# One output tile split into three single-bank tiles, block maxima split in two, and a new written-out order of the work

## The chip, the cores and the metric

The kernel runs on one core of a Trainium2 chip. The metric is the device time in microseconds (us) of one execution. The core has five engines that run side by side, each strictly in its own order: TensorE (PE, matrix products, with its weight loads shown as PEld), VectorE (DVE), ScalarE (ACT), GpSimd (POOL), and SyncE (SP), which here issues all DMAs. TensorE writes its results to PSUM, of which the kernel takes eight banks of 512 fp32 columns on 128 partitions.

## The reference

```python
# attention: q, k, v of (4 batches, 8 heads, 768 positions, 64)
scores = 1/sqrt(64) * q @ k.transpose
mask   = |block_i - block_j| <= 1, or first/last block on either side,
         or the block is one of 3 sampled blocks of its row   # blocks of 32
scores = where(mask, scores, -1e9) - rowmax
attn   = exp(scores) / (sum(exp(scores)) + 1e-9)
x      = (attn @ v) as (3072 tokens, 512)
# feed-forward: w_in (512, 2048), w_out (2048, 512)
h   = x @ w_in
out = (h * clip(h + 3, 0, 6) / 6) @ w_out
```

All arrays are fp32. The kernel keeps fp32 accuracy by splitting operands into a high part of type fp32r and a low part.

## The kernel before, in words

The work is cut into 64 *units*, 64 *steps* and 32 *weights*. They are Python objects whose methods each issue a few instructions, and the names of the methods are used below.

A **unit** `u0` to `u63` is one head of one batch and one half of its 384 query rows. On TensorE it has `m_0 m_1 m_2`, each two 128x384 score products for 128 query rows (384 keys each), from which DVE takes block maxima (`r_0 r_1 r_2`, one reduction over 768 columns each, 24 blocks of 32); `fin_0` adds the mask to the block maxima and `fin_1` reduces them to one negated row maximum. `mt` transposes that maximum with three small matmuls and `qm` (ACT) copies it into a row of the operand `qb`, so that the score products `s_0 s_1 s_2` (four matmuls each, of `KA,QA` and of `kb,qb`) come out already masked and shifted. From unit 10 on a DMA takes the place of `mt` and `qm`. `e_0 e_1 e_2` are the exponentials (ACT) and `av` the product with the values: in units 0 to 11 it also yields the row sums (12 matmul passes of 128 columns, `av_0 av_1 av_2`), later it runs in half the array. `qh kh qb` (ACT), `ql` (DVE) and `kl` (POOL, 1.8 us) make the high and low parts of the operands; `uc dw uu tt` and `ux` finish the unit's output.

A **weight** `w0` to `w31` is one 128-row chunk of `w_in` or `w_out`: a DMA load, `size` (ACT), `bits_0 bits_1 bits_2` (DVE), `high` (ACT), `low` (DVE), and a DMA that saves the low part to DRAM, from where the steps load it again.

A **step** `m0` to `m63` takes two of the 16 chunks of the feed-forward for one block of 384 tokens; eight steps make a block, and a block of tokens needs eight units. `h_00` to `h_11` are 24 matmuls, `ga gb gh gl` (ACT, DVE, ACT, POOL) the activation and its split, and `o_tj` 18 matmuls that accumulate into three output banks, one for each `t`, over all eight steps. After the last step of a block, `oc_t` (DVE, from bank `t`) and `od_t` (DMA) carry the block out.

**PSUM.** `big` is a pool of two tiles of two banks for `m`, `s`, `h` and a few others; `av` has one bank. The last three banks are one tile, `OUT` (line 370), of 128 x 3 x 512. Bank `t` of it is what `o_tj` accumulates into (line 850). Before the first step needs them, the same banks serve other purposes: `mq` (line 474) uses bank 2, and the `m` of units 1 to 8 (the `early` units, line 630) use banks 0 and 1 in place of a `big` tile, each `m_t` over both of them, so that `m_1` comes after `r_0` has read them and `m_2` after `r_1`.

**What sets the order.** No planner runs in the kernel. The string `SCORE` (line 41) lists all 3537 methods in one written-out order, `play` (line 886) calls them in that order, and every instruction is kept in program order on its engine (line 357, which is why the profile gives L357 for nearly all of them). So one phrase of `SCORE` places work on several engines' queues at once. The framework adds semaphore waits where an instruction touches a tile that another engine still uses.

Of the kernel before, what the change touches and what calls it, by code (L numbers as in the profile page):

```python
# [13 lines left out]
F32 = mybir.dt.float32  # L14
# [27 lines left out]
    u0 loadq loadk; k0 samp table ind ident; u0 loadv; w0 load; w2 load; u1 loadv; u0 qh qb ql kh; k0 index; u1 loadq;  # L42
    k0 allow_0 allow_1; u0 m_0; k0 allow_2; u0 m_1; k0 allow_3 indc; u0 r_0; k0 mq kb_0; w0 size; u0 r_1; k0 rows; w2
    size; k0 identc mqc; u0 kl m_2; k0 qb_00; u0 r_2; k0 qb_11; u1 qh qb; w0 bits_0; u1 loadk; k0 qb_01; w0 bits_1; k0
    qb_10; w0 bits_2; u0 fin_0; w0 high; w1 load; k0 kb_1; u0 fin_1 mt qm; w0 low; u0 s_0; u1 ql; w0 save; u0 s_1; w2
    bits_0; u2 loadq; u0 e_0; w2 bits_1; u1 kh; u0 av_0; w2 bits_2; u0 e_1; u1 kl; w3 load; u1 m_0; w2 high; u0 s_2;
    u1 r_0; w1 size; u0 av_1; w2 low; u2 loadk; u0 e_2; w1 bits_0; w2 save; u2 qh; u1 m_1; w1 bits_1; u0 av_2; u2 qb;
    w1 bits_2; u1 r_1; w1 high; w5 load; u2 loadv; w3 size; w1 low; u1 m_2; u0 dw; u2 ql; w1 save; u0 uc; u1 r_2; u3
    loadq; u2 kh; u1 fin_0; u2 m_0; u1 fin_1; u2 kl; u1 mt; u2 r_0; u1 qm s_0; w5 size; u2 m_1; w3 bits_0; u3 loadk;
    u1 e_0 s_1; w5 bits_0 bits_1; u1 s_2 e_1; w5 bits_2; u1 av_0 e_2; u2 r_1; w4 load; w5 high; w3 bits_1; u2 m_2; u3  # L50
    qh; u1 av_1; w5 low; u3 qb; u2 r_2; w5 save; u3 kh; u1 av_2; u3 ql; u2 fin_0; u4 loadq; u3 m_0; u2 fin_1; u3 kl;
    u1 dw; u3 loadv; u2 mt; u3 r_0; u2 qm; w4 size; u2 s_0; u1 uc; w4 bits_0; u3 m_1; u4 loadk; u2 s_1 e_0; u1 rg; w3
    bits_2; u3 r_1; w6 load; w3 high; u2 s_2; m1 loadout_0; u2 e_1 av_0; w4 bits_1; u2 e_2; w3 low; u3 m_2; w4 bits_2;
    u4 qh; w3 save; u2 av_1; u4 qb; u3 r_2; w7 load; w4 high; u2 av_2; u3 fin_0; u4 kh ql; u1 rc; u5 loadq; u4 kl; u3
    fin_1; w6 size; u1 rs; u3 mt; u4 m_0 loadv; u3 qm; u4 r_0; u2 uc; u3 s_0; u2 dw; u5 loadk; u3 s_1; w6 bits_0; u3
    e_0; w6 bits_1; u4 m_1; u3 e_1 s_2; w6 bits_2; u3 av_0; u4 r_1; w8 load; w6 high; u3 e_2; w6 low; u1 rb; u4 m_2;
    u5 qh; w4 low; u3 av_1; w6 save; u5 qb; u4 r_2; w4 save; w7 size; u3 av_2; u5 kh; u4 fin_0; u5 ql; u4 fin_1; u5
    kl; u6 loadq; u5 m_0; u3 uc; u5 loadv; u4 mt; u5 r_0; u3 dw; u4 qm; u3 rg; u5 m_1; w7 bits_0; w8 size; u4 s_0; u6
    loadk; w7 bits_1; m1 loadin_1; u4 s_1; m1 loadin_0; w8 bits_0; u4 e_0; w8 bits_1; u4 e_1 s_2; w8 bits_2; u4 av_0;
    u5 r_1; u4 e_2; w10 load; u6 qh; u1 ux_0; u5 m_2; u6 qb; u4 av_1; u6 ql; u1 ux_1; u5 r_2; u7 loadq; u6 kh; u4  # L60
    av_2; u5 fin_0; w8 high; u1 ux_2; u5 fin_1; u6 kl; u3 rc; u5 mt; u3 rs; u6 m_0; u4 uc; u6 loadv; u5 qm; u6 r_0;
    w10 size; u5 s_0; u7 loadk; w7 bits_2; u4 dw; u5 s_1 e_0; w10 bits_0; w9 load; u6 m_1; w10 bits_1; u5 e_1 s_2; u6
    r_1; u5 av_0; w7 high; w10 bits_2; u5 e_2; u3 rb; w8 low; u6 m_2; u7 qh; u5 av_1; u6 r_2; w8 save; u7 qb; w11
    load; u7 kh; u6 fin_0; u5 av_2; u7 ql; w10 high; u6 fin_1; u7 kl; u8 loadq; w9 size; u7 m_0 loadv; u5 uc; u6 mt;
    u7 r_0; u6 qm; u5 dw; u8 loadk; u6 s_0; w9 bits_0; u5 rg; w7 low; u6 s_1 e_0; u3 ux_0; w7 save; u7 m_1; u6 e_1
    s_2; w10 low; u6 av_0; u3 ux_1; w9 bits_1; w10 save; u6 e_2; w9 bits_2; u6 av_1; u8 qh; u7 r_1; w12 load; u8 qb
    kh; u3 ux_2; u6 av_2; u8 ql; w9 high; m1 loadout_1; u5 rc; u8 kl; u5 rs; w11 size; u7 m_2; u9 loadq; u8 loadv; u6
    uc; u7 r_2; u6 dw; u9 loadk; u7 fin_0; u8 m_0; u7 fin_1; w11 bits_0; u7 mt qm; u8 r_0; w12 size; u7 s_0; w9 low;
    u8 m_1; u7 e_0 s_1; w11 bits_1; w9 save; u5 rb; u7 s_2; u8 r_1; u7 e_1 av_0; w11 bits_2; u7 e_2; w12 bits_0; w14
    load; u9 kh; u8 m_2; w12 bits_1; u7 av_1; u9 qh; u8 r_2; u9 kl qb; w11 high; u7 av_2; u8 fin_0; u10 loadk; u8  # L70
    fin_1; u9 ql; u8 mt; u7 uc; u9 loadv; w11 low; u8 qm; u9 m_0; u10 loadq; u7 dw; u9 m_1 r_0; w11 save; w14 size; u7
    rg; u9 r_1; u8 s_0; u5 ux_0; u8 e_0 s_1; w12 bits_2; u5 ux_1; u8 s_2; w14 bits_0; w16 load; u8 e_1 av_0; u5 ux_2;
    u10 kh; w14 bits_1; u9 m_2; w14 bits_2; u8 e_2 av_1; u9 r_2; u10 kl; w18 load; u10 qh qb; u7 rc; u8 av_2; u7 rs;
    w12 high; w14 high; u9 fin_0; u11 loadk; u9 fin_1; u10 ql; u9 mt; u8 uc; u10 loadv; w12 low; u10 m_0; u11 loadq;
    u9 qm; u8 dw; u9 s_0; u10 r_0; w12 save; w16 size; w14 low; u9 s_1 e_0; w16 bits_0; w14 save; u9 e_1 s_2; w16
    bits_1; u7 rb; u9 av_0; w18 size; w16 bits_2; u9 e_2; w18 bits_0; w13 load; w18 bits_1; u10 m_1; u11 kh; u10 m_2;
    w18 bits_2; u9 av_1; u11 qh; u10 r_1; u11 kl; w15 load; w18 high; u9 av_2; u11 qb; u10 r_2; w16 high; w18 low; u12
    loadk; u9 uc; u11 loadv; u7 ux_0; w18 save; u9 dw; u10 fin_0; u7 ux_1; u9 rg; w16 low; w13 size; u7 ux_2; w16
    save; w13 bits_0; m0 h_00; w15 size; w13 bits_1; m0 h_10; w13 bits_2; w15 bits_0; w13 high; w17 load; m0 h_01; u10
    fin_1; w13 low; u10 mt; u11 ql; w13 save; m0 h_11; w15 bits_1; u12 loadq; m2 loadin_0; m1 h_00; u9 rc; m0 ga; w15  # L80
    bits_2; u9 rs; w19 load; m1 h_01; w15 high; m0 gb; m2 loadin_1; w15 low; m0 gh; m1 h_10; m3 loadin_0; w15 save;
    w17 size; m0 gl; m1 h_11; u10 s_0; m3 loadin_1; w17 bits_0; m1 ga; u9 rb; m0 o_00; w17 bits_1; m0 o_01; u10 e_0;
    m1 gb; m0 o_10; w19 size; w17 bits_2; u10 s_1; m1 gh; w19 bits_0; w20 load; u10 s_2; w19 bits_1; u10 e_1; m0 o_11;
    w19 bits_2; u12 kh; u11 m_0; m1 gl; w22 load; m0 o_20; w19 high; u11 r_0; w17 high; m0 o_21; m2 loadout_0; u10
    e_2; u11 m_1; w19 low; m2 loadout_1; u10 av_0; u12 qh; u9 ux_0; w19 save; u12 qb; u11 r_1; u12 kl; u11 m_2; u9
    ux_1; u10 av_1; w20 size; u11 r_2; w20 bits_0; u13 loadk; m2 h_00; w20 bits_1; w17 low; m2 h_01; w20 bits_2; w17
    save; w22 size; m2 h_10; u11 fin_0; w24 load; w20 high; w22 bits_0; m4 loadin_0; w22 bits_1; m2 h_11; u11 fin_1;
    w22 bits_2; u11 mt; m1 o_00; m2 ga; w20 low; w21 load; m1 o_01; m4 loadin_1; u12 ql; w20 save; w22 high; m1 o_10;
    m2 gb; u13 loadq; u12 m_0; m1 o_20; w22 low; m2 gh; u12 m_1 r_0; w22 save; w24 size; m2 gl; m1 o_11; m3 loadout_0;
    u12 r_1 m_2; m1 o_21; u12 r_2; u11 s_0; w21 size; m3 loadout_1; w24 bits_0; u11 s_1 e_0; u9 ux_2; u10 av_2; w21  # L90
    bits_0; u11 e_1; w21 bits_1; u11 s_2; w21 bits_2; u10 dw; u12 loadv; m2 o_00; u12 fin_0; w26 load; w21 high; u12
    fin_1; w24 bits_1; u12 mt; u10 uc; m2 o_01; u14 loadv; u13 kh; w24 bits_2; u11 av_0; w21 low; w23 load; u11 e_2;
    u13 kl; w21 save; u11 av_1; w24 high; u13 qh qb; u11 av_2; u13 ql; u14 loadk; w26 size; w24 low; u14 loadq; u12
    s_0; u11 uc; w26 bits_0; w24 save; u15 loadv; u11 dw; u13 m_0; w26 bits_1; m2 o_10; u12 e_0; u11 rg; w26 bits_2;
    m2 o_20; w23 size; u13 r_0; w25 load; m2 o_11; m4 loadout_0; w26 high; w23 bits_0; u13 loadv m_1; w23 bits_1; u12
    s_1; u13 r_1; m2 o_21; u12 e_1; w23 bits_2; u13 m_2; m4 loadout_1; u12 s_2; u13 r_2; w23 high; w28 load; u14 qh;
# [231 lines left out]
def fused_kernel(ctx: ExitStack, tc, qT, kT, vP, sampled, w_in, w_out, krows, table, ident_d, out):  # L328
# [81 lines left out]
    class Masks(Work):  # L410
# [11 lines left out]
        def heat(self):  # L422

            self.hot = sb.tile([P, 2, HALF], F32R, name="ghi")
            nc.gpsimd.memset(self.hot.bitcast(F32), 1.0)

        def warm(self, *number):
            for _ in range(number[-1]):
                pe.matmul(OUT[:, 2, :HALF], lhsT=self.hot[:, 0, :P], rhs=self.hot[:, 1], start=True, stop=True)

# [505 lines left out]
```

## Time and profile before

| | |
|---|---|
| time of 3 runs | 995.15 us median (993.82 to 997.5) |
| the profiled execution's own time | 994.87 us |
| its span, first to last instruction | 993.1 us |
| PE busy | 950.6 us, 96% of the span, 4756 matmuls |
| DVE busy | 642.3 us, 65%, 900 instructions |
| ACT busy | 471.1 us, 47% |
| POOL busy | 249.9 us, 25% |
| mean share of the DMA engines | about 0.75 in the first 160 us, 0.4 to 0.5 after it |

The profiled execution is the one that all rows below come from. Its own time is 1.8 us longer than its span (start and end of the program), and 0.3 us under the median. Busy time of PE overstates its work, since a record lasts until the modelled end of a matmul while the next one has begun. What a matmul costs in a dense row is read from the distance between starts.

### The profile page before, as it was taken

How to read it: one execution, taken by the hardware profiler on the slowest of the kernel's cores; microseconds unless marked ns; L12 is line 12 of the kernel's file. 1: busy time of each engine (PE TensorE's matmuls, PEld its weight loads, DVE VectorE, ACT ScalarE, POOL GpSimd, SP SyncE). 2: the span in 40 equal slices, each digit the busy share in tenths (PEclk: the TensorE clock that was granted, in tenths of full speed). 3: DMA queues.
4: the chain of work that ended last, by engine and by line, in shares of the span. 5: the costliest groups of instructions: out<-in, count | busy, mean ns of one | idle time of the engine just before them, and what ended most of it. 6: DMA issues, size and time to landing. Idle time of an engine off the chain costs nothing.

```text
span 993.1 us, 13262 instructions
## 1 busy us (share of the span) xinstructions
PE 950.6 (96%) x4756; PEld 767.9 (77%) x4756; DVE 642.3 (65%) x900; ACT 471.1 (47%) x712; POOL 249.9 (25%) x148
## 2 busy tenths in 40 slices
...
GB/s 199 193 244 210 273 267 236 202 220 147 144 139 139 123 165 132 155 111 165 142 153 132 131 152 163 124 154 134 170 147 108 149 131 138 145 48 146 142 118 72
DMA packets 103701, 155.48 MB, mean 157 GB/s; under 512 B 32819, under 2 KB 51891, under 8 KB 103636
## 3 DMA queue, kind: packets, MB, share of 16 engines
...
q14 instruction: 28, 0.23, 0.1%
...
## 4 chain that ended last, share of the span: by engine, by line
PE 80%; DVE 12%; ACT 3%; issue 3%; DMA 1%; POOL 0%; DVEq 0%; ACTq 0%
PE big L357 44%; PE out L357 25%; PE av L357 12%; DVE xhl L357 3%; DVE bm L357 3%; DVE acc L357 2%; DVE QA L357 2%; ACT pr L357 1%; ACT xhl L357 1%; DMA win_lo<-xhl 1%; DMA wout_lo<-xhl 1%; DVE wraw L357 0%; ACT qb L357 0%; DVE uu L357 0%; DMA qraw<-qT 0%
## 5 line engine op out<-in xcount | busy, mean ns | idle before, releaser
L357 PE MATMUL big<-xhl,win_hi 128*128 128x384 f32 x1024 | 265.0, 340 | 0.6 <-DVE bm L357 0.6
L357 POOL TENSOR_TENSOR glo<-g,ghi 128x768 fp32r<-128x768 f32 x64 | 120.2, 1878 | 430.3 <-ACT ghi L357 425.1
L357 ACT ACTIVATE pr<-big 128x768 f32<-128x768 f32 x192 | 153.0, 809 | 102.9 <-PE big L357 102.1
L357 POOL TENSOR_TENSOR kb<-kraw,KA 64x768 fp32r<-64x768 f32 x64 | 124.4, 1943 | 298.8 <-ACT KA L357 252.8
L357 PEld LDWEIGHTS big<-xhl,win_hi 128*128 128x128 f32 x1024 | 184.5, 188 | 14.3 <-issue 7.3
L357 DVE TENSOR_REDUCE bm<-big 128x24 f32<-128x768 f32 x168 | 158.0, 953 | 54.8 <-PE big L357 53.0
L357 PE MATMUL big<-xhl,wlo_in 128*128 128x384 f32 x512 | 172.3, 337 | 0.0
L357 PE MATMUL av<-pr,vo 128*64 128x384 f32 (+1 forms) x768 | 163.6, 494 | 0.1
L357 PE MATMUL out<-wout_hi,ghi 128*128 128x512 f32 x384 | 152.7, 398 | 5.8 <-DVE wraw L357 5.8
L357 PE MATMUL out<-wout_hi,glo 128*128 128x512 f32 x384 | 151.2, 394 | 0.6 <-POOL glo L357 0.6
L357 PE MATMUL out<-wlo_out,ghi 128*128 128x512 f32 x384 | 150.8, 393 | 0.0
L357 PE MATMUL big<-QA,KA 128*128 128x384 f32 x384 | 138.5, 361 | 3.1 <-ACT pr L357 1.3
L357 PE MATMUL big<-qb,kb 97*128 97x384 f32 x384 | 132.7, 345 | 3.9 <-ACT qb L357 3.2
L357 DVE SCALAR_TENSOR_TENSOR g<-g,big 128x768 f32<-128x768 f32 x64 | 60.8, 950 | 109.7 <-ACT g L357 109.3
L357 ACT ACTIVATE g<-big,half_b 128x768 f32<-128x768 f32 x64 | 57.7, 902 | 142.5 <-PE big L357 126.9
L357 PEld LDWEIGHTS av<-pr,vo 128*64 128x64 f32 (+1 forms) x768 | 67.6, 147 | 65.6 <-issue 50.5
L357 PE MATMUL big<-KA,QA 128*128 128x384 f32 x336 | 92.7, 367 | 13.9 <-ACT KA L357 5.1
L357 PEld LDWEIGHTS big<-KA,QA 128*128 128x128 f32 x336 | 74.8, 255 | 35.9 <-issue 8.8
L357 DVE TENSOR_TENSOR acc<-pr 128x768 f32<-128x768 f32 x52 | 54.3, 1045 | 68.1 <-ACT pr L357 67.8
L357 PEld LDWEIGHTS big<-xhl,wlo_in 128*128 128x128 f32 x512 | 96.2, 188 | 0.0
L357 PEld LDWEIGHTS big<-QA,KA 128*128 128x128 f32 x384 | 73.9, 192 | 23.8 <-ACT pr L357 7.7
L357 ACT CAST ghi<-g 128x768 fp32r<-128x768 f32 x64 | 53.3, 833 | 73.7 <-DVE g L357 48.5
...
## 6 DMA issues: line engine op xcount, KB each, us to landing
...
```

Of the source, the lines that this page charges most:

```text
L357: return lambda *a, **k: tc.keep_in_program_order(op(*a, **k))
```

## The change

Three things are changed. The tile `OUT` becomes three tiles of one bank each, `out0`, `out1` and `out2`, taken from the pool anew by each use. The `m` of an early unit takes two of these tiles, one for each of its two matmuls, and the pair of banks turns with the unit: units 1 and 2 have banks 1 and 2, units 3 and 4 banks 2 and 0, units 5 and 6 banks 0 and 1, units 7 and 8 banks 1 and 2. Each early `r` becomes two reductions over 384 columns, one a bank. And `SCORE` is another order of the same 3537 methods. Two methods that no `SCORE` calls (`heat` and `warm`) go.

```diff
-    OUT = outp.tile([P, NT, DM], F32, name="out")
...
         def mq(self):
-            self.mqp = OUT[:, 2]
+            self.mqp = outp.tile([P, DM], F32, name="out0")
...
         def m(self, t):
             if self.early:
-                ps = OUT[:, 0:2]
+                bank = (self.n - 1) // 2
+                ps = [outp.tile([P, DM], F32, name=f"out{(bank + 1 + j) % NT}")[:, :HALF] for j in range(2)]
             else:
                 ps = big_tile()
-            self.mps = [*(self.mps if t else []), ps[:, :, :HALF]]
+            self.mps = [*(self.mps if t else []), ps if self.early else ps[:, :, :HALF]]
             for j in range(2):
-                pe.matmul(ps[:, j, :HALF], lhsT=self.QA[:, t:HALF:NT], rhs=self.KA[:, j * HALF:(j + 1) * HALF], start=True, stop=True)
+                out_j = ps[j] if self.early else ps[:, j, :HALF]
+                pe.matmul(out_j, lhsT=self.QA[:, t:HALF:NT], rhs=self.KA[:, j * HALF:(j + 1) * HALF], start=True, stop=True)
 
         def r(self, t):
             if t == 0:
                 self.bm = sb.tile([P, NT, NB], F32, name="bm")
             bm = self.bm[:, t].rearrange("p (j n) -> p j n", j=2)
-            dve.tensor_reduce(out=bm, in_=self.mps[t].rearrange("p j (n e) -> p j n e", e=BLK), axis=AX.X, op=ALU.max)
+            if self.early:
+                for j in range(2):
+                    dve.tensor_reduce(out=bm[:, j], in_=self.mps[t][j].rearrange("p (n e) -> p n e", e=BLK), axis=AX.X, op=ALU.max)
+            else:
+                dve.tensor_reduce(out=bm, in_=self.mps[t].rearrange("p j (n e) -> p j n e", e=BLK), axis=AX.X, op=ALU.max)
...
-                moe_out[self.b, self.hf] = [OUT[:, t_] for t_ in range(NT)]
+                moe_out[self.b, self.hf] = [outp.tile([P, DM], F32, name=f"out{t_}") for t_ in range(NT)]
```

Of the two orders, this is what the engines' queues hold around unit 4 and 5, read from the strings (the diff of the strings themselves is some 570 lines):

```
before  PE   u4.s_0 u4.s_1 u4.s_2 u4.av_0 u5.m_2 u4.av_1 u4.av_2 u5.mt u6.m_0 u5.s_0 u5.s_1 u6.m_1
after   PE   u4.mt u5.m_0 u5.m_1 u4.s_0 u5.m_2 u4.s_1 u4.s_2 u4.av_0 u4.av_1 u4.av_2 u5.mt u6.m_0 u6.m_1 u5.s_0
before  DVE  u5.r_0 w7.bits_0 w7.bits_1 w8.bits_0 w8.bits_1 w8.bits_2 u5.r_1 u1.ux_0 u6.ql u5.r_2 u5.fin_0 u1.ux_2 u5.fin_1 u3.rc u6.r_0
after   DVE  w7.low w8.bits_2 u5.r_0 u5.r_1 u1.ux_0 u5.r_2 u5.fin_0 u1.ux_2 u5.fin_1 w8.low u6.ql w10.bits_0 w10.bits_1 u3.rc w10.bits_2 u6.r_0
after   ACT  u3.uc u4.qm u3.dw w8.high u4.e_0 u4.e_1 u1.ux_1 u4.e_2 u6.qh u6.qb w10.size w9.size u6.kh u4.uc u5.qm
```

The pattern of the new order, `mt` of a unit, then `m_0 m_1` of the next, then `s_0` of the first, with `r_0 r_1` side by side, is the same from unit 1 to unit 8. Up to `u9 s_0` TensorE's queue holds the same 97 methods in both orders, and DVE's holds eight more in the new one (`w14 low`, the four DVE methods of `w16`, `w18 bits_0 bits_1`, `u10 r_0`). Up to `u1 s_0` it holds three more (`w3 bits_0 bits_1 bits_2`). Up to `m7 o_21` TensorE's and ACT's queues hold the same methods in both. The last 17 methods of `SCORE` are the same, in the same order:

```
m62 o_21; m63 o_00 o_01 o_10 oc_0 o_11 od_0 o_20 oc_1 o_21 od_1 oc_2 od_2
```

## Rows read from the trace of the kernel before

**Rows 1.** Busy time by stretch: length, then engine busy (instructions), clock, DMA share, GB/s.

```profile
0.00:29.41 29.41, 17.65 (x59) 12.85 (x59) 18.12 (x35) 16.55 (x27) 10.28 (x23) 0.97 0.66 204
29.41:103.89 74.48, 65.85 (x266) 47.46 (x265) 62.23 (x102) 58.81 (x97) 16.33 (x9) 0.97 0.70 215
103.89:230.25 126.36, 120.07 (x584) 96.74 (x584) 110.21 (x164) 74.70 (x118) 32.08 (x16) 1.00 0.74 238
230.25:993.10 762.85, 747.05 (x3852) 610.84 (x3850) 451.79 (x602) 321.07 (x471) 191.21 (x101) 1.00 0.45 136
```

**Rows 2.** Timeline: first matmul of `u1 s_0`, `u9 s_0` and `m7 o_21`.

```profile
29.41 0.63 PE L357 MATMUL big<-QA,KA 128*128 128x384 f32 x1
...
103.89 0.44 PE L357 MATMUL big<-QA,KA 128*128 128x384 f32 x1 [0.59 <-ACT qb L357]
...
230.25 0.39 PE L357 MATMUL out<-wout_hi,ghi 128*128 128x512 f32 x1
```

**Rows 3.** Chain of waits, pieces without a wait: start, length, what, matmuls.

```profile
79.62 3.87 PE av L357 x12
...
889.72 11.93 PE big L357 x66
...
974.95 10.31 PE out L357 x45
```

**Rows 4.** Who waited for whom, 29.41 to 103.89: total, times, longest.

```profile
PE big L357 <- ACT qb L357: 3.0, 6, 0.6
PE out L357 <- DVE bm L357: 2.0, 2, 1.1
...
DVE bm L357 <- PE out L357: 7.3, 9, 1.4
```

**Rows 5.** Chain of waits around `u4 m_0`, `r_0`, `m_1`.

```profile
56.89 0.36 PE out L357 x2
...
57.28 0.97 DVE bm L357
...
58.29 0.68 PE out L357 x2
```

**Rows 6.** The tile bm: count, shortest, median, longest in ns, first and last start.

```profile
L357 DVE TENSOR_REDUCE mneg<-bm x64: 185/228/230, 14.8 to 874.7; 128x3 fp32r<-128x72 f32 x64
L357 DVE TENSOR_REDUCE bm<-out x24: 948/956/961, 21.7 to 91.0; 128x24 f32<-128x768 f32 x24
```

**Rows 7.** DVE timeline: `bits_0`, two `bits`, and `low` of weights.

```profile
59.43 0.43 DVE L357 TENSOR_SCALAR xhl<-xhl 128x512 int32<-128x512 int32 x1
59.89 1.42 DVE L357 SCALAR_TENSOR_TENSOR xhl<-wraw,xhl 128x512 int32<-128x512 int32 x2
...
70.48 0.69 DVE L357 TENSOR_TENSOR xhl<-xhl,win_hi 128x512 f32<-128x512 f32 x1
```

**Rows 8.** The tile QA on DVE, and the timeline around two `kl` on POOL.

```profile
L357 DVE SCALAR_TENSOR_TENSOR QA<-qraw,QA x64: 555/556/3877, 3.8 to 866.2; 64x384 fp32r<-64x384 f32 x64
...
72.94 1.81 POOL L357 TENSOR_TENSOR kb<-kraw,KA 64x768 fp32r<-64x768 f32 x1 [6.12 <-ACT KA L357]
73.09 2.07 DVE L357 SCALAR_TENSOR_TENSOR QA<-qraw,QA 64x384 fp32r<-64x384 f32 x1
...
56.01 1.82 POOL L357 TENSOR_TENSOR kb<-kraw,KA 64x768 fp32r<-64x768 f32 x1 [6.24 <-ACT KA L357]
```

**Rows 9.** Who waited for whom on PE, 230.25 to the end.

```profile
PE out L357 <- DVE wraw L357: 5.8, 6, 1.7
PE big L357 <- DVE QA L357: 3.6, 3, 1.6
PE big L357 <- DVE bm L357: 1.7, 2, 1.6
```

**Rows 10.** Timeline of the last block's `o_10`, `oc_0`, `o_11`.

```profile
984.86 0.39 PE L357 MATMUL out<-wout_hi,glo 128*128 128x512 f32 x1
...
985.28 0.69 DVE L357 COPY wraw<-out 128x512 f32<-128x512 f32 x1 [7.82 <-PE out L357]
...
986.03 0.50 PE L357 MATMUL out<-wout_hi,ghi 128*128 128x512 f32 x1 [0.78 <-DVE wraw L357]
```

More of the change, by code (lines that the diff above doesn't have):

```diff
@@ L41 @@
 SCORE = """
[L42 to L96, printed above, removed]
@@ L102 @@
-    m4 h_01; u15 kh; u13 sumb; w30 load; w25 high; u15 m_0; m6 loadin_0; u13 av sumc; u15 kl r_0; u14 s_0; u13 tt; u11
-    ux_0; u16 loadk; u17 loadv; m4 h_10; w25 low; u14 e_0; u13 uu; w25 save; u15 m_1; w28 bits_2; m4 h_11; u15 r_1;
-    w27 load; w28 high; m3 o_10; m4 ga; w28 low; u14 s_1; w28 save; m4 gb; m3 o_20; u14 e_1; w26 low; u14 s_2; m5
-    loadout_0; m4 gh; u14 suma; w26 save; u15 m_2; m3 o_11; w30 size; u15 r_2; m4 gl; u16 kh; m3 o_21; m5 h_00; u16
-    qh; m5 loadout_1; u16 qb; w30 bits_0; m5 h_01; u11 ux_1; u15 fin_0 fin_1; u16 kl; u14 e_2; u15 mt; m4 o_00; w27
@@ L107 @@
-    size; m6 loadin_1; m7 loadin_0; u14 av sumb; u17 loadk; u14 sumc; u11 ux_2; m5 h_10; u14 tt; u18 loadv; u16 ql;
-    u14 uu; u17 loadq; m5 h_11; w27 bits_0 bits_1; u16 m_0; m5 ga; m4 o_01; w30 bits_1; m4 o_10; m5 gb; m4 o_20; u16
-    r_0; m5 gh; u16 m_1; m6 loadout_0; m4 o_11; m5 gl; u16 r_1 m_2; m4 o_21; u16 r_2; u15 s_0; w30 bits_2; u15 s_1
-    e_0; u16 fin_0; w29 load; w27 bits_2; m5 o_00; w30 high; u16 fin_1; w31 load; u15 s_2; w27 high; w30 low; u16 mt;
-    m5 o_01; u15 e_1; w27 low; w30 save; m5 o_10; u17 kh; w27 save; u15 suma; m6 h_00; u17 qh kl qb; m6 h_10; u15 e_2;
@@ L222 @@
-    loadk qb; u45 loadv; m31 o_01; u41 sumc tt uu; u43 m_2; m32 h_00; u44 ql; u43 r_2; u45 loadq; m32 h_10; u43 fin_0
-    fin_1; m31 oc_0; u43 mt; m32 h_01; u44 kh; m31 od_0; m32 h_11; m34 loadin_0; u44 kl; m31 o_10; m32 ga; m34
-    loadin_1; m31 o_11; m32 gb; u45 loadk; m31 o_20 oc_1; u44 m_0; m32 gh; m33 loadout_0; u43 s_0; u44 r_0; m31 od_1;
-    m32 gl; m31 o_21; u43 e_0; u44 m_1; m31 oc_2; m33 loadout_1; u43 s_1; u44 r_1; m31 od_2; m32 o_00; u43 e_1; m32
-    o_10; u43 suma s_2; m33 h_00; u43 e_2; u45 kh; u43 sumb; m33 h_01; u45 qh; u43 sumc; m32 o_01; m35 loadin_0; u45
@@ new lines @@
+    size; k0 rows; w2 size; k0 mqc; u0 kl m_2; k0 qb_01; u0 r_2; k0 qb_11 qb_10; w2 bits_0; u1 loadk qh; w2 bits_1; u1
+    qb; k0 qb_00; w2 bits_2; w0 bits_0; w1 load; w2 high; u1 ql; u0 fin_0; u2 loadq; w0 bits_1 bits_2; k0 kb_1; u0
+    fin_1; w0 high; w3 load; u0 mt; u1 kh; w0 low; u0 qm; w2 low; u1 m_0; w0 save; u1 m_1 kl r_0; w2 save; u0 s_0; w1
+    size; u0 s_1 e_0; u1 r_1 m_2; u0 e_1 s_2; u2 loadk; w1 bits_0; u1 r_2; u0 av_0; u2 qh qb ql; u0 e_2 av_1; w1
+    bits_1; u3 loadq; w3 size; w1 bits_2; u0 av_2; u1 fin_0; w1 high; w5 load; u1 fin_1; w3 bits_0; w1 low; u1 mt; u0
@@ new lines @@
+    bits_1; u7 qh; u3 rb; u5 av_1; u7 qb ql; w11 size; w9 bits_2; u8 loadq; u5 av_2; w11 bits_0; w9 high; w12 load;
+    w11 bits_1; u7 kh; w11 bits_2; u6 mt; u7 loadv; u5 uc; u7 m_0; w10 low; w14 load; u7 m_1; u6 qm; u7 kl r_0; w10
+    save; u5 dw; u6 s_0; w11 high; u5 rg; u6 s_1; u7 r_1; u6 e_0; u7 m_2; u8 loadk; u3 ux_0; u6 e_1 s_2; u7 r_2; u6
+    av_0; u3 ux_1; u8 qh; u3 ux_2; u8 qb; u7 fin_0; u6 av_1; u7 fin_1; u6 e_2; w11 low; u8 ql; w12 size; w11 save; u6
+    av_2; w9 low; u9 loadq; w14 size; u5 rc; w9 save; w14 bits_0; u7 mt; u5 rs; u8 kh; w12 bits_0; u8 loadv; w12
@@ new lines @@
+    bits_1; u6 uc; u8 m_0 m_1; u7 qm; u8 kl r_0; u6 dw; u7 s_0; u8 r_1; u7 s_1 e_0; u8 m_2; u9 loadk; w12 bits_2; u7
+    e_1 s_2; u8 r_2; w16 load; w12 high; u7 av_0; u5 rb; u9 qh; u8 fin_0 fin_1; u9 qb ql; u7 av_1 e_2; w14 bits_1; u10
+    loadq; w14 bits_2; u7 av_2; w12 low; w14 high; w18 load; w14 low; w12 save; u9 kh; u8 mt; u9 loadv; w14 save; u7
+    uc; u9 m_0 kl; u8 qm; u9 r_0; u7 dw; u9 m_1; w16 size; u9 r_1; u7 rg; u8 s_0; u10 loadk; u5 ux_0; u8 e_0 s_1; w16
+    bits_0; u5 ux_1; u8 s_2; w16 bits_1; u8 e_1 av_0; w16 bits_2; u10 qh; u5 ux_2; w13 load; w16 high; u10 ql; u9 m_2;
```

488 lines of the change are left out of this document (267 added, 221 removed).

## The prediction, on record before the changed kernel ran

> **What bounds the kernel now.** I first cut the windows view at three places that the two orders share [rows 1], found as instructions in the timeline [rows 2]: `u1 s_0` (29.41 us), `u9 s_0` (103.89) and `m7 o_21` (230.25). The reader is to see that PE is nearly full after 230 us (747.05 of 762.85) and has gaps before. In the second stretch DVE is busy 62.23 of 74.48 us, PE 65.85 by records that overstate it, ACT 58.81: three engines that wait for each other.
>
> PE's own work comes from the dense pieces of the chain of waits [rows 3]: 0.18 us a 384-column matmul (11.93 / 66), 0.23 us a 512-column one (10.31 / 45), 3.87 us for the twelve `av` matmuls of an early unit. An early unit has 12 `s` and 6 `m` matmuls, so 18 x 0.18 + 3.87 = 7.1 us, its three small transposes left out. The second stretch holds eight units: 74.48 / 8 = 9.3 us a unit, of which PE stands 2.2. Then I read who waited there [rows 4]. PE waits for the `qb` copy behind `mt` (3.0 us in 6 waits) and for the maxima (2.0 in 2). DVE waits at `r` for PE's `m` (7.3 in 9).
>
> Last I read PE's waits after 230 us [rows 9]. The largest is for `wraw`, which is `oc`: 5.8 us in 6. The timeline shows what kind of wait it is [rows 10]. The last matmul of `o_10` starts at 984.86, so `o_11` was due at 985.09. It starts at 986.03, as `oc_0` ends. But `o_11` writes bank 1 and `oc_0` reads bank 0. They share only the tile `OUT`, and the wait belongs to the tile. `oc_0` in turn starts only after `o_10`, which it doesn't read.
>
> **The change, part by part.**
>
> *Three tiles for one.* A write to one bank no longer waits for a read of another. At the end both orders hold the same methods, so nothing there but the tiles can take the wait away. Four of the six waits are of this kind in the last two blocks, where PE has no attention work left to put between: 986.03 - 985.09 = 0.94 us each, 3.8 us. What is late next there is `o_21`, then `oc_2` and its DMA, as now. The other two lie inside attention work (the longest 1.7 us [rows 9], so 5.8 - 4 x 0.78 = 2.7 together) and I take half, 1.3. Sum -5.1, between -6.9 and 0 if the wait stays.
>
> *One maximum a bank.* It adds 24 DVE instructions. No row shows a 384-column reduction. From the 72-column one (228 ns) and the 768-column one (956) [rows 6] the slope is 728 / 696 = 1.05 ns a column, so 228 + 312 x 1.05 = 0.55 us each, 1.11 for 0.96. From below it is half of 956, nothing added. I take 0.15 us a pair as the dearer end, 21 pairs in the second stretch: 3.2 us of DVE. In return `m_1` starts sooner. Before, `m_0` to the next pair is 58.29 - 56.89 = 1.40 us, with the maximum of 0.97 between [rows 5]. After, the first half starts 0.18 us sooner, at 57.28 - 56.89 - 0.18 = 0.21, ends at 0.76, and `m_1` may start at 0.80. The second half ends at 1.32, so `m_1` is through at 1.54. PE's own work in that is 4 x 0.18 = 0.72, so the turn costs PE 0.8 us a unit.
>
> The Trainium skill has a rule that weighs here (Perfetto Trace Analysis, Optimizing Scalar/DVE Operations). A DVE instruction has a fixed access cost, about 125 ns on PSUM, so larger operations pay where the engine is saturated. Where it isn't but holds others up, smaller pieces can end the work sooner. By the first half the 21 pairs cost 2.6 us and return nothing, which is the first rival below; by the second the turn counts.
>
> *The new order, first stretch.* DVE now does `w2`, parts of `w0` and `u1 ql` ahead of `u0 fin_1`, some 2.4 us more by the durations of [rows 7]. But `u1 m_0 m_1` stand ahead of `u0 s_0` on PE, and three more `bits` are done by `u1 s_0`. I take 0, from -1 to +2.4.
>
> *Second stretch.* In the new order `m_0 m_1` of the next unit stand between `mt` and `s_0`, so the turn of 0.8 us covers the `qb` copy, which cost up to 0.6 each time. `r_0 r_1` are side by side, so DVE doesn't stop between them, and 5.3 us of PE work (`s`, `m_2`, `av`) lie between `m_2` and `mt`. That gives 7.1 + 0.8 = 7.9 us a unit. I add 0.2 for the small transposes, 0.2 for `m_0` waiting on `kh`, which is late in ACT's queue behind two `size`, and 0.4 for DVE held by POOL. The price of that is in [rows 8]: a `ql` that starts 0.15 us into `kl` takes 2.07 us and not 0.56, 1.5 us more, and I count one in four. 8.7 x 8 = 69.6 us. DVE is the check. By `u9 s_0` it has eight more methods behind it: 0.69 (`w14 low`), 0.43 + 1.42 + 0.69 (`w16`), 0.43 + 0.71 (`w18`), 0.96 (`r_0`), 5.3 us [rows 6, 7]. Three `bits` (1.85) went ahead of the stretch. 62.23 + 5.3 - 1.85 + 3.2 = 68.9. An engine that stood 12.2 us before won't be without a gap, so I take 72: -2.5, between -8.5 (66, halves at half the price) and +6 (every unit held 1.5 us).
>
> *Third stretch.* PE and ACT have the same left, DVE 5.3 us less. DVE is busy 110.21 of 126.36 here and the chain of waits runs mostly over weights. I take 3 of the 5.3. Bounds -5.3 and +2, the latter if the DMA engines, at 0.74, hold the weights instead.
>
> *Fourth stretch.* PE is full, and the other waits on DVE are 3.6 + 1.7 us [rows 9]. An order drawn anew can meet as many others. I take nothing for it, between -3 and +4.
>
> SP's queue is reordered too. No `load` becomes a new wait by name, and the DMA shares of [rows 1] leave room, so I cost it at nothing. If that is wrong it shows as PE waiting for `KA`.
>
> **Sum.** 0 - 2.5 - 3.0 - 5.1 = -10.6 us against the profiled execution's own 994.87 (span 993.1 and 1.8 around it): 984.3. That execution lies 0.3 us under the median of 995.15, so by the median 984.5.
>
> **The rivals.**
> *DVE is the bound early, and the order returns nothing.* The split costs 3.2 us in the second stretch, and what was gained is waited for in the third. Only the tiles pay: 994.87 - 5.1 = 989.8. For it: DVE at 62.23 of 74.48. Against it: 7.3 us of DVE's gaps there are waits for `m`.
> *The tiles don't separate.* The wait stays, on the pool's release or on PE's own order, and the order alone pays: 994.87 - 5.5 = 989.4. Against it: [rows 10], two banks and one tile.
> *Slower: DVE held by POOL.* In the new order DVE's instruction ahead of `r_0` is a weight's, near the moment when `kh` lets `kl` start. If it starts just after, it takes 1.5 us longer, `r_0` is late, and PE stands in front of `m_1` with nothing to do. The forecast has 0.4 of this a unit. In every unit it is 1.1 x 8 = 8.8 us more, the third stretch loses its 3, and a `ql` in the fourth stretch that is caught (3.6 us in 3 now) is caught nine times, 7 us more: 984.3 + 18.8 = 1003. It decides from some 10 more held instructions than forecast. For it: [rows 8]. Against it: `kl` also ran from 56.01 to 57.83 beside a maximum of unchanged 0.97 us [rows 5], and the new order puts `r_0 r_1` behind `kh`.
> The Trainium skill states that mechanism (SBUF — State Buffer, Who interferes with whom): a DVE instruction with two SBUF inputs and a GpSimd instruction that reads SBUF exclude each other for a whole instruction, and `tensor_reduce` never contends. By that rule, with which both rows agree, the early maxima are safe and the weights are not.
> *All goes well.* 66 us in the second stretch, all 5.3 in the third, all 6.9 for the tiles: 994.87 - 20.7 = 974.
>
> **How the numbers follow.** Forecast 0.45 (980 to 989); DVE bound 0.22; tiles don't separate 0.12; held by POOL 0.11; all well 0.10. About 0.5% (5 us) is what a measurement can tell from no change. Faster by more than that, under 990.2, are the forecast (0.44), all well (0.10) and somewhat over half of the two cases near 989.6 (0.18): 0.72. Slower is the held case, 0.11; 0.17 is left for the same. The range 975 to 997 leaves out the held case and the best half of the last one.
>
> **What would show it.** Right: no PE wait for `wraw` in the last two blocks; the gap after `mt` gone and one of 0.3 to 0.5 us in front of each half of `m_1`; `u9 s_0` near 101 and `m7 o_21` near 225. Wrong: `QA`, `xhl` or `bm<-bm,mq` on DVE at 1.5 to 2 us beside `kb` again and again before 100 us; PE waiting for `bm` or `KA` more than 1 us a unit; or more than 6 us of PE waits on DVE after 230 us.

## The result: 0.6% slower, and the profile after

The changed kernel takes 1003.25 us (median of 20 runs, 996.05 to 1007.09); the kernel before, run beside it, 997.5 (20 runs). The ratio is 1.0058, 95% interval 1.0044 to 1.0071. The forecast was 984.5.

To read the rows it must be known that the profiled execution is the fastest of the 20, with its own time of 996.05 us and a mean granted clock of 0.998; the mean clock of all 20 is 0.992. So the profile shows only a part of the loss.

The windows of the kernel after, cut at the same three instructions as [rows 1] (`u1 s_0`, `u9 s_0`, `m7 o_21`), with the same columns:

```profile
0.00:31.22 31.22, 17.81 (x60) 13.06 (x61) 19.84 (x43) 18.14 (x29) 11.33 (x23) 1.00 0.60 194
31.22:105.94 74.72, 64.77 (x264) 45.82 (x263) 66.24 (x124) 59.28 (x98) 15.98 (x8) 1.00 0.76 232
105.94:235.00 129.06, 122.15 (x583) 97.95 (x584) 114.27 (x159) 73.55 (x115) 31.40 (x17) 0.99 0.69 222
235.00:994.20 759.20, 746.01 (x3852) 611.96 (x3850) 458.13 (x601) 319.96 (x471) 194.47 (x101) 1.00 0.45 136
```

| stretch | before | after | difference | forecast |
|---|---|---|---|---|
| first | 29.41 | 31.22 | +1.8 | 0 |
| second | 74.48 | 74.72 | +0.2 | -2.5 |
| third | 126.36 | 129.06 | +2.7 | -3.0 |
| fourth | 762.85 | 759.20 | -3.7 | -5.1 |

`u9 s_0` is at 105.94 and `m7 o_21` at 235.00, where the forecast had 101 and 225. The sum is +1.0 in this execution. The median lies 7.2 us above it; most of that part goes with the clock, as far as the runs show (below).

Who waited on PE and DVE between `u1 s_0` and `u9 s_0` (total, times, longest), to be held against [rows 4]:

```profile
PE out L356 <- DVE bm L356: 8.1, 6, 2.3
DVE bm L356 <- PE out L356: 3.5, 5, 1.0
...
PE big L356 <- ACT qb L356: 1.1, 2, 0.6
```

The waits for `qb` went from 3.0 us in 6 to 1.1 in 2, as forecast. The waits for the maxima went from 2.0 in 2 to 8.1 in 6. The longest, 2.3, is not the turn of the forecast. It stands in the timeline at `u5` (start, length, engine, tiles, and in brackets the idle time before and who ended it):

```profile
58.66 0.69 PE L356 MATMUL out<-KA,QA 128*128 128x384 f32 x2
58.69 1.88 POOL L356 TENSOR_TENSOR kb<-kraw,KA 64x768 fp32r<-64x768 f32 x1 [8.60 <-ACT KA L356]
58.82 2.30 DVE L356 SCALAR_TENSOR_TENSOR xhl<-wraw,xhl 128x512 int32<-128x512 int32 x1
...
61.04 2.17 DVE L356 TENSOR_REDUCE bm<-out 128x12 f32<-128x384 f32 x4
...
61.64 0.97 PE L356 MATMUL out<-KA,QA 128*128 128x384 f32 x2 [2.29 <-DVE bm L356]
```

`m_0` starts at 58.66 and `kl` at 58.69. DVE starts `w8 bits_2` at 58.82, ahead of `r_0`, and it takes 2.30 us where its median is 0.69. `r_0` starts only at 61.04 and PE stands 2.29 us in front of `m_1`. The same happens with `w4 bits_1` and `w3 low`, and PE stands 2.21 and 2.09 us:

```profile
38.20 2.28 DVE L356 SCALAR_TENSOR_TENSOR xhl<-wraw,xhl 128x512 int32<-128x512 int32 x1
...
48.33 2.31 DVE L356 TENSOR_TENSOR wlo_out<-xhl,wout_hi 128x512 fp32r<-128x512 f32 x1
```

Held instructions are not new. In the same stretch the kernel before has three that take over 0.3 us more than usual (at 38.39, 73.09 and 92.01), the kernel after four. New is that three of the four stand just ahead of `r_0`; before, PE never stood more than 1.14 us there.

The reductions, by the tile `bm` (shortest, median, longest in ns):

```profile
L356 DVE TENSOR_REDUCE bm<-big x168: 887/957/960, 6.3 to 881.6; 128x24 f32<-128x768 f32 x168
...
L356 DVE TENSOR_REDUCE bm<-out x48: 542/550/558, 18.7 to 91.2; 128x12 f32<-128x384 f32 x48
```

The half costs 550 ns; the estimate was 0.55 us [rows 6]. It was never lengthened beside POOL.

The last block, the place of [rows 10]:

```profile
987.79 0.69 DVE L356 COPY wraw<-out 128x512 f32<-128x512 f32 x1 [7.85 <-PE out L356]
987.83 0.39 PE L356 MATMUL out<-wlo_out,ghi 128*128 128x512 f32 x1
...
988.06 0.40 PE L356 MATMUL out<-wout_hi,glo 128*128 128x512 f32 x1
...
988.29 0.39 PE L356 MATMUL out<-wout_hi,ghi 128*128 128x512 f32 x1
```

`oc_0` (987.79) starts while `o_10` still runs, and `o_11` follows it 0.23 us on (988.06 to 988.29). The wait of 0.94 is gone.

### The profile page after: what moved, and what is told of

Read it like the earlier page. It is cut to its first block, busy times and chain, and to the rows that moved or that the text cites. A ratio compares the mean times of both kernels' runs of the same rounds, so it can differ in the third digit from the quotient of the medians.

```text
span 994.2 us, 13284 instructions
## 1 busy us (share of the span) xinstructions
PE 950.7 (96%) x4756; PEld 768.8 (77%) x4756; DVE 658.5 (66%) x924; ACT 470.9 (47%) x712; POOL 253.2 (25%) x148
## 4 chain that ended last, share of the span: by engine, by line
PE 78%; DVE 12%; issue 4%; ACT 3%; DMA 2%; SPq 1%; DVEq 0%; ACTq 0%
PE big L356 44%; PE out L356 25%; PE av L356 9%; DVE xhl L356 4%; DVE bm L356 2%; DVE acc L356 2%; DVE QA L356 2%; ACT pr L356 1%; DMA wraw<-w_in 1%; DMA qb<-mneg 1%; ACT KA L356 1%; SPq L356 1%; DVE g L356 0%; ACT xhl L356 0%; ACT QA L356 0%
## 5 line engine op out<-in xcount | busy, mean ns | idle before, releaser
L356 POOL TENSOR_TENSOR kb<-kraw,KA 64x768 fp32r<-64x768 f32 x64 | 127.6, 1994 | 321.9 <-ACT KA L356 286.6
L356 PEld LDWEIGHTS big<-xhl,win_hi 128*128 128x128 f32 x1024 | 184.7, 188 | 16.4 <-issue 4.3
L356 PEld LDWEIGHTS big<-KA,QA 128*128 128x128 f32 x336 | 74.7, 255 | 33.5 <-issue 10.6
L356 DVE TENSOR_TENSOR acc<-pr 128x768 f32<-128x768 f32 x52 | 56.7, 1091 | 64.9 <-ACT pr L356 64.7
```

Source lines behind the costliest of these rows:

```text
L356: return lambda *a, **k: tc.keep_in_program_order(op(*a, **k))
```

## The experiments

Each kernel ran beside the kernel before. Ratios are to that; "clock" is the mean granted clock of all its runs. The three lengths are stretches one to three of its profiled execution.

| kernel | median us (runs) | ratio (95%) | clock | stretches, us |
|---|---|---|---|---|
| before | 994.5 to 997.5 | 1 | 0.995 to 0.996 | 29.4, 74.5, 126.4 |
| after | 1003.25 (20) | 1.0058 (1.0044 to 1.0071) | 0.992 | 31.2, 74.7, 129.1 |
| tiles_only | 991.45 (7) | 0.9942 (0.992 to 0.9963) | 0.995 | 29.5, 75.7, 126.3 |
| order_only | 1015.07 (6) | 1.0178 (1.0149 to 1.0207) | 0.990 | 32.4, 82.4, 128.9 |
| early_new | 1002.29 (12) | 1.0055 (1.0035 to 1.0075) | 0.991 | 31.7, 82.7, 129.5 |
| late_new | 993.13 (12) | 0.997 (0.995 to 0.999) | 0.995 | 31.1, 75.7, 129.1 |
| late_tiles | 990.86 (12) | 0.9945 (0.9922 to 0.9968) | 0.996 | 29.9, 76.1, 127.9 |
| r0_first | 999.23 (12) | 1.0017 (0.9994 to 1.004) | 0.994 | 32.4, 79.0, 129.3 |
| after_warm | 999.85 (12) | 1.0041 (1.0022 to 1.006) | 0.997 | 31.4, 78.0, 129.2 |
| after_nokl | 992.56 (12) | 0.9973 (0.9954 to 0.9992) | 0.997 | 32.7, 71.6, 129.9 |
| low_later | 995.12 (12) | 0.9996 (0.9979 to 1.0013) | 0.997 | 32.7, 72.6, 129.7 |
| low_later_old | 993.58 (12) | 0.9975 (0.9962 to 0.9989) | 0.996 | 32.7, 71.5, 128.1 |

**tiles_only: the tiles and the split, with the order of before.**

```diff
 # the changed kernel, but
-SCORE = """ (the new order) """
+SCORE = """ (the order of before) """
```

> The three tiles and the split maxima, with the order of before. Theory (the new order loses early by DVE held behind kl, and the tiles pay at the end): no PE wait for wraw after 230 us, 3 to 5 us less in the last 760 us; the split costs at most 3 us early; ratio to before 0.995 to 0.999. Rival (the 24 more DVE instructions and the waits of m between banks are what costs): m7 o_21 later than 233 us, ratio 1.002 to 1.006.

0.58% faster than before by the ratio, 4.9 us by the medians, and somewhat better than expected. All that PE still waited for after `m7 o_21` (total, times, longest):

```profile
PE big L357 <- DVE QA L357: 3.5, 3, 1.6
PE big L357 <- DVE bm L357: 2.8, 4, 1.6
PE big L357 <- DVE acc L357: 0.5, 1, 0.5
```

The 5.8 us for `wraw` of [rows 9] are gone, and only 1.1 us more of waits for the maxima took their place: the fourth stretch is 757.92, 4.9 us shorter. So the tiles do separate, and the loss is in the order.

**order_only: the kernel before in the new order.** One tile `OUT`, whole maxima; `r_t` of an early unit stands ahead of `m_(t+1)`, which no engine's queue notices.

```diff
 # the kernel before, but
-SCORE = """ (the order of before) """
+SCORE = """ (the new order, in units 1 to 8 with r_0 ahead of m_1, r_1 ahead of m_2) """
```

> The new order with the one tile and the whole maxima of before; each engine's queue is that of the changed kernel. Theory: the waits for wraw stay, the held DVE instructions stay, and m_1 waits for a whole maximum: slower than the changed kernel by 3 to 6 us, ratio to before 1.008 to 1.013. Rival (the split is what costs, the order is good): ratio under 1.003.

1.8% slower, more than expected. Between `u1 s_0` and `u9 s_0`:

```profile
PE out L356 <- DVE bm L356: 13.1, 7, 2.8
```

Against after's 8.1 in 6, every `m_1` waits for a whole maximum, on top of the held weights. Some 0.55% of the 1.2% between the two kernels is the tile of the steps, by late_tiles below; the rest says that the new order needs the split.

**early_new and late_new: one half of the new order each.** The splice is in step 8, where both orders have issued the same set of 1023 methods.

```diff
 # the changed kernel, but with A the order of before, B the new one
+SCORE = B[:1023] + A[1023:]   # early_new
+SCORE = A[:1023] + B[1023:]   # late_new
```

> Changed code, new order up to the point in step 8 where both orders have issued the same methods, then the order of before. Theory (the loss is early): m7 o_21 at 234 to 236 us as in the changed kernel, the end 4 us better by the tiles, ratio to before 1.000 to 1.004. Rival (the loss, in the runs of low clock above all, is in the order after step 8): ratio 0.995 to 0.998.

> Changed code, order of before up to that point in step 8, the new order after it. Theory (the loss is early): m7 o_21 at 230 to 233 us and ratio to before 0.995 to 0.999. Rival (the loss is in the new order after step 8): ratio 1.004 to 1.008, with the granted clock of most runs near 0.99 as in the changed kernel.

The early half alone takes all of the loss (1.0055 against 1.0058), more than expected of it. The late half is 0.28% dearer than tiles_only by the medians of the ratios, whose intervals overlap: some 3 us. (low_later and low_later_old, below, differ in the same late part by 0.21%.) In early_new the granted clock falls too. Its windows, the second stretch first and then four cuts in it (length, busy of the five engines, clock, DMA share, GB/s):

```profile
31.70:114.40 82.70, 71.09 (x264) 52.49 (x262) 68.27 (x124) 59.83 (x98) 15.57 (x8) 0.90 0.68 209
40.80:47.60 6.80, 6.13 (x18) 5.66 (x19) 5.90 (x13) 2.92 (x5) 0.00 (x0) 0.50 0.77 235
64.70:68.10 3.40, 3.40 (x11) 3.16 (x11) 1.76 (x5) 2.26 (x4) 0.00 (x0) 0.50 0.78 231
85.20:88.60 3.40, 3.40 (x12) 3.40 (x12) 1.91 (x5) 2.02 (x3) 0.00 (x0) 0.50 0.59 188
95.40:98.80 3.40, 3.40 (x11) 3.20 (x12) 1.90 (x4) 0.81 (x1) 0.00 (x0) 0.50 0.41 130
```

At 0.50 TensorE runs at 1.2 GHz. PE had stood 2.21, 2.29, 2.39 and 1.90 us in front of `m_1`, until 41.5, 62.9, 83.9 and 95.2, each time behind a held weight; the first fall comes 0.7 us before the stand ends, the others 0.2 to 1.8 us after it. This is the same stretch of code that took 74.7 us at clock 1.00 in the profile of after. Of the 8.0 us between the two, PE's waits for the maxima make 1.6 (9.7 against 8.1); 17 us of the stretch ran at the lower clock.

**late_tiles: the tiles only where `o` needs them.** The order of before; the early units keep one tile of banks and whole maxima.

```diff
 # the kernel before, but
-    outp = ctx.enter_context(tc.tile_pool(name="outp", bufs=1, space=bass.MemoryType.PSUM))
+    early_pool = ExitStack()
+    outp = early_pool.enter_context(tc.tile_pool(name="outp", bufs=1, space=bass.MemoryType.PSUM))
+    late = []
...
-                moe_out[self.b, self.hf] = [OUT[:, t_] for t_ in range(NT)]
+                if not late:
+                    early_pool.close()
+                    late.append(ctx.enter_context(tc.tile_pool(name="outl", bufs=1, space=bass.MemoryType.PSUM)))
+                moe_out[self.b, self.hf] = [late[0].tile([P, DM], F32, name=f"out{t_}") for t_ in range(NT)]
```

> Order of before, one tile and whole maxima for the early units as before, three tiles only for the output of the steps. Theory: the split maxima cost about 1.4 us by u9 s_0 (105.3 against 103.9 us with tiles and split), so this gets u9 s_0 at 103.9 again, no wait for wraw, and ratio to before 0.993 to 0.995, up to 1.5 us under the run with the split. Rival (the early waits between banks gain something): slower than that run, ratio 0.996 or more.

0.9945 against 0.9942, and `u9 s_0` at 106.0, not at the expected 103.9: with the order of before, splitting the early maxima neither gains nor costs anything that can be measured.

**r0_first, after_warm and after_nokl: three ways at the held weight.** Each is the changed kernel with one thing altered.

```diff
 # r0_first: the held weight operation of units 3, 4, 5, 7, 8 goes behind r_1; at unit 5:
-    u5 loadv; w8 bits_2; w7 save; u3 uc; u5 m_0 m_1; u4 qm; u5 kl r_0; w9 load; u3 dw; u4 s_0; w8 high; u3 rg; u5 r_1
+    u5 loadv; w7 save; u3 uc; u5 m_0 m_1; u4 qm; u5 kl r_0; w9 load; u3 dw; u4 s_0; u3 rg; u5 r_1; w8 bits_2
 # after_warm: in m, behind m_0 of units 2 to 8
+            if self.early and self.n > 1 and t == 0:
+                spare = outp.tile([P, DM], F32, name=f"out{bank % NT}")[:, :HALF]
+                for _ in range(6):
+                    pe.matmul(spare, lhsT=self.QA[:, t:HALF:NT], rhs=self.KA[:, :HALF], start=True, stop=True)
 # after_nokl: in kl
+            if 2 <= self.n <= 8:
+                return
```

> The changed kernel, but the weight instruction that was held behind kl just ahead of r_0 (units 3, 4, 5, 7, 8) comes after r_1 in DVE's order. Theory (a weight instruction that starts just behind kl holds r_0, m_1 and so PE, and the clock falls after it): no PE stand over 1.2 us in front of m_1, u9 s_0 at 98 to 103 us, clock 1.00 from 48 to 104 us, ratio to before 0.994 to 0.999. Rival (the new order loses by its pattern, m_0 and m_1 together in front of s_0): u9 s_0 still at 106 to 114, ratio 1.004 to 1.008.

> The changed kernel with six more matmuls (1.1 us) behind m_0 of units 2 to 8 that write the third output bank, which nothing reads: they fill the time in which PE stands in front of m_1. Theory (the lower clock of most runs comes from PE standing there): clock 1.00 from 48 to 104 us in nearly all of that stretch, mean clock of the runs 0.995 or more, time 2 to 5 us under the changed kernel's. Rival (the clock falls for another reason, or costs nothing): mean clock near 0.991 as in the changed kernel, time the same or up to 5 us above it.

> The changed kernel without kl in units 2 to 8: the low part of the keys is left out there (it keeps that of an earlier unit). Theory (DVE held by POOL is the early loss): no DVE instruction more than 0.3 us over its usual time from 28 to 104 us, u9 s_0 at 98 to 102 us, ratio to before 0.992 to 0.998. Rival (the pattern of the order, or the split, is the loss): u9 s_0 at 105 us or later, ratio 1.003 or more.

*after_nokl* leaves the low part of the keys out in units 2 to 8. No weight is held between 31 and 102 us, PE's waits for the maxima are

```profile
PE out L356 <- DVE bm L356: 3.8, 7, 0.8
```

and the kernel comes from 1.0058 to 0.9973 with the clock at 0.997. It names POOL's `kl` as what holds DVE. `u9 s_0` is at 104.3 and not under 102 as expected, since the first stretch stays long (32.7).

*after_warm* still has the holds, but PE has six unread matmuls to do in them: at `u5` its stand is 1.22 us and not 2.29. In its profile the four cuts of above are at full clock, which alone shows little, since after's own profile is at full clock there too:

```profile
40.80:47.60 6.80, 6.39 (x26) 4.89 (x27) 6.46 (x15) 4.66 (x9) 0.00 (x0) 1.00 0.66 214
64.70:68.10 3.40, 3.40 (x14) 2.28 (x13) 2.23 (x6) 3.31 (x6) 0.00 (x0) 1.00 0.62 186
85.20:88.60 3.40, 3.40 (x13) 1.88 (x11) 3.30 (x9) 3.31 (x6) 0.00 (x0) 1.00 0.32 102
95.40:98.80 3.40, 3.40 (x12) 1.83 (x12) 3.03 (x7) 2.55 (x6) 0.00 (x0) 1.00 0.66 228
```

Its 12 runs have clocks of 0.995 to 0.999; of after's 20, 16 lie under 0.995. So it is PE's standing there that costs the clock. In time it is 0.17% better than after by the ratios, whose intervals overlap. There are 42 extra matmuls of 0.18 us, and five units are held in its profile, not three; that these take back what the clock gives is likely but not shown.

*r0_first* has no held weight, but new stands. At `u6`:

```profile
68.83 0.83 ACT L356 CAST KA<-kraw 128x768 fp32r<-128x768 f32 x1 [2.37 <-DMA kraw<-kT]
...
69.71 0.94 PE L356 MATMUL out<-KA,QA 128*128 128x384 f32 x2 [3.07 <-ACT KA L356]
```

The load of the keys landed late (5.9 us from issue to landing, where the median of its `kraw` loads is 3.8), PE stood 3.07 us, and the clock was at 0.51 from 69.9 to 76.8. So this run mixes two things: `r_0` is never held, as expected, but `u9 s_0` (111.4) and the time (1.0017) come out later than its theory said. Whether moving `bits`, which read the load buffer, made the transfer late, it can't say.

**low_later and low_later_old: the same cure without touching a load buffer.** In units 3, 4, 5, 7 and 8 a `low` goes behind `r_1`, so that the weight operation ahead of `r_0` is gone or 0.69 us earlier. low_later_old has the order of before from step 8 on.

```diff
-    u5 kh; u4 mt; w7 low; u5 loadv; w8 bits_2; w7 save; u3 uc; u5 m_0 m_1; u4 qm; u5 kl r_0; ... u5 r_1
+    u5 kh; u4 mt; u5 loadv; w8 bits_2; u3 uc; u5 m_0 m_1; u4 qm; u5 kl r_0; ... u5 r_1; w7 low save
```

> The changed kernel, in its own order but for five low parts of weights: in units 3, 4, 5, 7 and 8 one `low` (of w5, w3, w7, w10, w9) that stood ahead of r_0 on DVE, with its save, now stands behind r_1. The weight's operation that was held by kl so comes 0.69 us sooner, or is no longer there. It differs from the run that moved `bits` in that a `low` doesn't read the loaded weight, so no load buffer comes free later and the `kh` of the next units isn't delayed. Theory that DVE held by POOL is the loss: no weight operation of over 1.5 us ahead of r_0 in units 3 to 8, PE stands at most 1 us in front of m_1, no wait of PE for KA over 1 us, u9 s_0 at 100 to 104 us, time 990 to 996 us. Rival, that the order itself is the loss wherever a weight's work is put: u9 s_0 at 106 or later, time 998 to 1003 us.

> The same as the run beside it up to the place in step 8 up to which both orders have issued the same set of methods, and from there the order of before. If the early order is good once nothing is held, and the late part of the new order costs 2 to 3 us: 987 to 992 us, the best of all. If the early order gains nothing even so: 992 to 996 us, no better than the new tiles with the order of before (991.45).

At `u5` in low_later:

```profile
60.03 0.69 PE L356 MATMUL out<-KA,QA 128*128 128x384 f32 x2 [1.88 <-ACT KA L356]
60.06 1.81 POOL L356 TENSOR_TENSOR kb<-kraw,KA 64x768 fp32r<-64x768 f32 x1 [8.44 <-ACT KA L356]
...
60.58 2.18 DVE L356 TENSOR_REDUCE bm<-out 128x12 f32<-128x384 f32 x4 [2.17 <-PE out L356]
...
61.20 0.97 PE L356 MATMUL out<-KA,QA 128*128 128x384 f32 x2 [0.47 <-DVE bm L356]
...
62.00 0.34 PE L356 MATMUL big<-QA,KA 128*128 128x384 f32 x1
```

`r_0` runs beside `kl` at its usual pace and PE stands 0.47 in front of `m_1`; so it is in all units from 3 to 8. Moving five subtractions on DVE, with their saves, takes the kernel from 1.0058 to 0.9996 and the clock from 0.992 to 0.997. Here too one load of keys was late (PE stood 1.88 in front of `m_0`, where at most 1 us was expected), so that wait isn't peculiar to r0_first.

`u9 s_0`, at 105.4, lies between what the two theories said; the time, 995.12, is within what the theory of held weights gave. For low_later_old the second of its two cases came, 993.58: with nothing held, the new early order is still 0.33% dearer than the order of before under the same tiles (0.9975 against 0.9942; the intervals only touch). Its windows show where, to be held against tiles_only's 29.5, 75.7 and 126.3:

```profile
0.00:32.68 32.68, 19.09 (x61) 14.18 (x61) 19.84 (x43) 18.16 (x29) 11.34 (x23) 1.00 0.59 189
32.68:104.15 71.47, 66.38 (x264) 47.39 (x263) 62.03 (x124) 59.54 (x98) 16.02 (x8) 0.98 0.78 241
104.15:232.28 128.13, 120.05 (x584) 97.00 (x585) 115.22 (x159) 73.84 (x115) 31.52 (x17) 1.00 0.70 223
```

The second stretch gains 4.3 us, the first loses 3.2 and the third 1.8.

The fastest kernels are tiles_only and late_tiles, 0.55 to 0.58% under the kernel before and about 1.1% under the changed one.

## Why the prediction was wrong

**The step that failed** is the second stretch's allowance of 0.4 us a unit "for DVE held by POOL", counted at one unit in four, with no term for what such a stand does to TensorE's clock. In the profiled execution three units of eight were held, each with PE standing 2.1 to 2.3 us; 3 x (2.2 - 0.47) = 5 us of standing more than without a hold (0.47 each in low_later), where the allowance was 0.4 x 8 = 3.2, and the stretch took 74.7 us for the 72 forecast.

**The turn** in the same stretch was sized too low. Without the holds the stretch takes 71.5 (low_later_old) to 72.6 (low_later), some 8.9 us a unit; the prediction's 8.7 without its 0.4 is 8.3. From `m_0` to `s_0` it is 1.97 us in low_later (60.03 to 62.00) and not 1.54. The prediction took 56.89 for the start of `m_0` before [rows 5]. That is only where the chain of waits enters it; in the timeline `m_0` starts at 56.44:

```profile
56.44 0.80 PE L357 MATMUL out<-KA,QA 128*128 128x384 f32 x2
```

So it is luck that 72, which the prediction reached by allowing for DVE's gaps, lies near the stretch without holds. Right were the `qb` wait gone, the split at 0.55 us a half, and a gap of 0.47 us in front of `m_1`.

**The miss in parts.** The profiled execution is 11.6 us over the forecast: 1.8 in the first stretch, 2.7 in the second, 5.7 in the third, 1.4 in the fourth. The median adds 7.2.

**The clock** was in no term and no rival. A 384-column matmul of a dense row starts 0.32 us after the last where the granted clock is 0.50, as here in early_new, and 0.18 where it is 1.00:

```profile
42.41 0.53 PE L356 MATMUL big<-QA,KA 128*128 128x384 f32 x1
42.73 0.53 PE L356 MATMUL big<-qb,kb 97*128 97x384 f32 x1
```

The same two distances stand in the kernel after, on either side of 22.86. There the trace has its first record of the clock, a rise; ahead of it the windows view prints 1.00 without a record:

```profile
20.28 0.53 PE L356 MATMUL big<-QA,KA 128*128 128x384 f32 x1
20.60 0.53 PE L356 MATMUL big<-qb,kb 97*128 97x384 f32 x1
...
23.21 0.34 PE L356 MATMUL big<-QA,KA 128*128 128x384 f32 x1
23.39 0.34 PE L356 MATMUL big<-qb,kb 97*128 97x384 f32 x1
```

The mean clock of after's runs is 0.992, 0.006 under the profiled one. At a loss of half a clock that is 0.006 / 0.5 x 994 = 12 us more at the lower level; where PE is dense about half of it is lost, some 6 of the 7.2 us between the profile and the median. This is worked out, not measured. A line through after's 20 runs gives 0.7 us for each 0.001 of clock, some 4 us for the same 0.006, and two of its runs at 0.997 took 1000.30 and 1000.68. So some 4 to 6 of the 7.2 go with the clock, and what the rest is stays open. Not each stand is followed by a fall: the profile of after has three stands of over 2 us before 65 us, and its clock there stays at 1.00; it is the run of the highest clock and the fastest. Nor does each fall need such a stand: the one of 108.2 in after has none of over 0.75 us in the 40 us ahead of it.

The Trainium skill has a rule on this that the prediction left out (TensorE: Matmul & The Clock Gate, Part 1): an idle window of TensorE brings its clock to half, and that window is free-running, so that one kernel differs from run to run. The runs agree with the second part: 0.987 to 0.998 for the same kernel. Whether stands as short as these make up such a window, no run here shows.

**The first stretch** was costed at 0 with a bound of +2.4, "some 2.4 us more" of DVE work ahead of `u0 fin_1`. The bound came true. PE's wait for the row maximum in front of `u0 mt`, before and after:

```profile
PE big L357 <- DVE mneg L357: 3.3, 1, 3.3
...
PE big L356 <- DVE mneg L356: 5.6, 1, 5.6
```

The three `bits` done earlier gave nothing back. All kernels with the new early order have 31.2 to 32.7 here. Of those with the old one three have 29.4 to 29.9 and late_new 31.1, so one execution of this stretch is good to 1 or 2 us. Part of that is the moment of the clock's first rise: 22.9 us in the trace of after and 25.7 in that of low_later, where the stretch is 32.7. With the rise at 22.4 to 22.9 the old order has 29.5 (tiles_only) and 29.9 (late_tiles), the new one 31.2 (after), so some 1.5 us is the order's. No run undid this part by itself.

**The third stretch** was to give 3 us and took 2.7, the largest part of the miss in the profile. DVE has five fewer instructions in it (159 for 164), yet 114.27 us of busy time for 110.21 [rows 1]. Twelve of its instructions are held by over 0.3 us there in every kernel with the new early order, seven or eight with the old one; in after they take 16.4 us more than usual, in the kernel before 10.6. So the less work on DVE that the forecast counted on didn't come: no kernel with the new early order has less than 128.1 us here. But tiles_only and late_new, which run the same order through it, took 126.3 and 129.1, so how much of the 2.7 is the order's stays open.

**The tiles** were right: -5.1 forecast, -4.9 in the fourth stretch and 0.58% in the time of tiles_only. **The fourth stretch** of the new order gives back about 1.3 of it in this execution, within the -3 to +4 that was left to it; low_later, with the same late order, has 757.63 us there and gives back nothing.

**The rivals.** The slower one, DVE held by POOL, named the mechanism, the place and the very instruction ("DVE's instruction ahead of `r_0` is a weight's"). It got 0.11 because `kl` was seen beside an unlengthened maximum [rows 5, 8], but that row speaks for reductions, not for weights, as its own sentence on the Trainium skill (SBUF — State Buffer, Who interferes with whom) said. The trace agrees with that rule again: operations with two inputs in SBUF take 2.3 us for 0.69 when they start behind `kl`, reductions beside it never lengthen. Its sum (1003) came out near by luck, for another reason than it gave: three to five held units and the clock, not eight held units. "DVE is the bound early" (989.8) is near what the new tiles with the old order measure (991.45), but not by that mechanism.
